# A talking-heads attention with a Fourier mix: the Fourier transform folded a second time, with other changes of order and transfer

## The chip, the cores and the metric

The kernel runs on one core of a Trainium2 chip. The metric is the time of one execution in device microseconds (us), and the median of several executions is taken. The core has five engines that work side by side, each with an instruction stream of its own: TensorE for matmuls (PE in the profile, with its loads of stationary weights as PEld), VectorE (DVE), ScalarE (ACT), GpSimd (POOL) and SyncE (SP), which here only issues transfers. Transfers are also issued by GpSimd, and with the change by ScalarE.

## What is computed

Everything is fp32. Attention over 8 batches, 12 heads, 448 rows and 64 elements per head is followed by a Fourier mix and a feed-forward block (cut):

```python
scores = scale * q @ k.T                           # b, h, i, j
scores = einsum('bhij,hg->bgij', scores, w_pre)    # "premix" over heads
attn = exp(scores - max) / (sum + 1e-09)
attn = einsum('bhij,hg->bgij', attn, w_post)       # "postmix" over heads
x = (attn @ v), heads side by side                 # 8 x 448 x 768
u = x + real(fft(fft(x, axis=1), axis=2))          # the Fourier mix
un = (u - mean) / sqrt(var + 1e-06)
out = u + relu(un @ w_ch1) @ w_ch2                 # 768 -> 3072 -> 768
```

The real part of the two transforms is cos(rows) x cos(columns) minus sin(rows) x sin(columns). Cosines are even and sines odd, so a row and its mirror image can be added or subtracted first, and only half the sums are needed: this is folding.

## The kernel before

The mixing phase goes through 192 steps, 24 for each batch. A step gathers scores for a few rows of all heads (Kr), mixes the heads (mx), takes maximum and exponential (PP), scales them on GpSimd, mixes again (po) and turns the result (Pv). Other work is dealt among the steps by the tables AT_*, counted from the start of a batch: transposes of q and k (AT_T), the scores (AT_QK), attention times v (AT_AV), transposes of the result into X (AT_X), the transform over rows (AT_Z, emit_z) and that over columns (AT_S, emit_s2). The pool named ms holds four PSUM tiles, mx has one of two banks. The Fourier work of a batch comes 14 or more steps after the batch has ended, and so among the steps of the next one.

X is folded once in each direction on GpSimd (pairs, even, odd). TensorE, VectorE and ScalarE take their instructions in the order of emission; GpSimd and SyncE get theirs from a scheduler. The result u goes to a DRAM tensor per batch; groups of rows that are held in reversed order are scattered to it row by row by an indirect transfer. After that a feed-forward phase reads u again. Weights are also split into parts and summed in advance (wts), one VectorE operation in a step.

```python
AT_T = ((7, 0), (18, 18), (15, 17))
AT_QK = ((0, 2, 2), (0, 1, 2), (0, 1, 2), (0, 1, 2),
         (0, 1, 2), (1, 1, 2), (0, 1, 2), (0, 1, 2))
AT_AV = ((0, 2, 4), (0, 1, 4), (3, 4, 5), (2, 3, 4))
AT_X = (11, 20, 25, 29)
AT_Z = (38, 38, 38, 38, 42, 42, 42)
AT_S = ((41, 44), (49, 53))
    # ... cut
    def emit_tables():
        for t, n in ((rows, "at"), (ts, "ts"), (tce, "tc"), (tdo, "td")):
            nc.sync.dma_start(out=t, in_=cn[n].ap())
    # ... cut
                nc.gpsimd.dma_start(
                    out=t[64 * y:64 * y + 64, :, x, :],
                    in_=src[b, 6 * y + 2 * xx + x].rearrange("(p c) d -> p c d", c=C7))
    # ... cut
    def emit_premix(T):
        mx = pmx.tile([P, 2, 512], F32, name="mx", tag="mx")
        Kr = steps[T]["Kr"]
        for x in range(2):
            for z in range(2):
                nc.tensor.matmul(mx[64 * z:64 * z + 64, x, :S],
                                 kw1[64 * x:64 * x + KR, :],
                                 Kr[64 * x:64 * x + KR, z, :], start=True, stop=True)
        steps[T]["mx"] = mx
    def emit_max(T):
        nmx = psm.tile([P, 2], F32, name="nmx", tag="nmx")
        for x in range(2):
            nc.vector.tensor_reduce(nmx[:, x:x + 1], steps[T]["mx"][:, x, :S],
                                    axis=AX.X, op=ALU.max, negate=True)
        steps[T]["nmx"] = nmx
    def emit_exp(T):
        PP = ppp.tile([P, 2, S], F32, name="PP", tag="PP")
        den = psm.tile([P, 2], F32, name="den", tag="den")
        for x in range(2):
            nc.scalar.activation(PP[:, x, :], steps[T]["mx"][:, x, :S], ACTF.Exp,
                                 bias=steps[T]["nmx"][:, x:x + 1],
                                 accum_out=den[:, x:x + 1])
        steps[T]["PP"], steps[T]["den"] = PP, den
    # ... cut
        for x in range(2):
            nc.gpsimd.tensor_scalar(PP[:, x, :], PP[:, x, :], rcp[:, x:x + 1], 1.0,
                                    op0=ALU.mult, op1=ALU.mult)
    # ... cut
        def pairs(op, h):
            if h == 0:
                box.append(pxs.tile([GR + 1, DM], F32, name="xs", tag="xs"))
            h = slice(h * DH, (h + 1) * DH)
            nc.gpsimd.tensor_tensor(box[-1][:n, h], Xa[:n, h], Xb[:n, h], op=op)
        def even():
            xs = box[-1]
            nc.gpsimd.tensor_copy(out=xe[:n, 0:DH + 1:DH], in_=xs[:n, 0:DH + 1:DH])
            nc.gpsimd.tensor_tensor(xe[:n, 1:DH], xs[:n, 1:DH], xs[:n, DM - 1:DH:-1],
                                    op=ALU.add)
        def odd():
            xd = box[-1]
            nc.gpsimd.tensor_tensor(xo[:n, :], xd[:n, 1:DH], xd[:n, DM - 1:DH:-1],
                                    op=ALU.subtract)
        folds.extend([lambda: pairs(ALU.add, 0), lambda: pairs(ALU.add, 1), even,
                      lambda: pairs(ALU.subtract, 0), lambda: pairs(ALU.subtract, 1),
                      odd])
        batches[g["b"]]["xf", pair] = (xe, xo)
    # ... cut
    def emit_z(b, par, ch):
        d0, w = (EVEN, ODD)[par][ch]
        ps = ms_tile()
        for pair, n in enumerate(PR):
            nc.tensor.matmul(ps[:w, :SH + 1],
                             batches[b]["xf", pair][par][:n, d0:d0 + w],
                             ts[:n, pair, par, :], start=(pair == 0), stop=(pair == 1))
        z = pzz.tile([w, SH + 1], F32, name=f"z{par}{ch}", tag=f"z{par}{ch}")
        batches[b]["z", par, ch] = z
        return [lambda: copy(ENG["z"], z[:, :], ps[:w, :SH + 1])]
    def emit_s2(b, pair, par):
        st = batches[b]
        n, i0 = PR[pair], pair * GR
        chunks, tab = ((EVEN, tce), (ODD, tdo))[par]
        ps = ms_tile()
        for ch, (_, w) in enumerate(chunks):
            nc.tensor.matmul(ps[:n, :DH + 1], st["z", par, ch][:, i0:i0 + n],
                             tab[:w, ch, :],
                             start=(ch == 0), stop=(ch == len(chunks) - 1))
        def done():
            for back in range(2):
                X = groups[b * NG + 2 * pair + back]["X"]
                m = GR if back else n
                sub, add = (ALU.subtract, ALU.add) if par else (ALU.add, ALU.add)
                if back:
                    sub, add = add, sub
                nc.vector.tensor_tensor(X[:m, 0:DH + 1], X[:m, 0:DH + 1],
                                        ps[:m, 0:DH + 1], op=sub)
                nc.vector.tensor_tensor(X[:m, DH + 1:DM], X[:m, DH + 1:DM],
                                        ps[:m, DH - 1:0:-1], op=add)
            if par == 0:
                return
            for back in range(2):
                X = groups[b * NG + 2 * pair + back].pop("X")
                if back:
                    nc.gpsimd.indirect_dma_start(
                        out=u_scr[b][:, :],
                        out_offset=bass.IndirectOffsetOnAxis(
                            ap=rows[:GR, pair:pair + 1], axis=0),
                        in_=X[:GR, :], in_offset=None)
                    continue
                nc.sync.dma_start(out=u_scr[b][i0:i0 + GR, :], in_=X[:GR, :])
                if n > GR:
                    nc.sync.dma_start(out=u_scr[b][i0 + GR:i0 + n, :], in_=X[GR:n, :])
        return [done]
    # ... cut
    ET = mybir.EngineType
    with tc.manual_schedule(engines={ET.PE, ET.DVE, ET.Activation}):
        while s < TOT or any(fill.values()):
            take("none", s)
            if 0 <= s + LM < TOT:
                emit_premix(s + LM)
                emit_max(s + LM)
            flush()
            if 0 <= s + LM < TOT:
                emit_exp(s + LM)
            if 0 <= s < TOT:
                emit_postmix(s)
            take("AV", s)
            if 0 <= s < TOT:
                emit_turn(s)
            if s >= 4:
                wts.deal(1)
            if 0 <= s + LM < TOT:
                emit_scale(s + LM)
            if folds:
                folds.pop(0)()
            take("QK", s)
            if 0 <= s + LG < TOT:
                if any(e[2] is not None and e[2] <= (s + LG) // BS for e in pend):
                    flush()
                emit_gather(s + LG)
            take("full", s)
            s += 1
        flush()
        wts.deal(1000)
    # ... cut
    def load_u(t):
        us[t] = pu.tile([P, NT2, DM], F32, name=f"u{t}", tag=f"u{t}")
        for x in range(NT2):
            p = 0
            while p < P:
                b, r = divmod(t * TB + x * P + p, S)
                n = min(P - p, S - r)
                nc.sync.dma_start(out=us[t][p:p + n, x, :], in_=u_scr[b][r:r + n, :])
                p += n
```

## Time and profile before

The time is 2514.99 us, the median of 3 executions (2512.84 to 2515.37). The profiled execution has a span of 2513.7 us.

| what | value |
|---|---|
| PE busy | 2412.0 us, 96% of the span |
| PEld busy | 1552.2 us, 62% |
| DVE, ACT, POOL busy | 1498.9, 794.2 and 636.0 us |
| mean granted clock of TensorE | 0.990 |
| moved by transfers | 373.01 MB, 148 GB/s |
| first premix (line 425) | starts at 48.69 us |
| first feed-forward matmul (line 834) | starts at 966.7 us |
| matmul instructions of emit_z (line 570) | 224 |
| matmul instructions of emit_s2 (line 584) | 224 |
| GpSimd additions of 384 elements (line 547) | 64 of 1003 ns |

How to read the profile: an engine's busy time counts from the start of an instruction to its end. Matmuls are pipelined, so that they overlap, and the distance between their starts tells more of their cost than their duration does. A row of a view in order of time has start, time taken, engine, line of the program, operation, the tile written and those read, and in brackets how long the engine was idle and what ended that. The chain follows what ended last back to what released it, step by step. "Issue" is time in which nothing that the profile shows was waited for.

### The profile page before, as it was taken

The numbers are of one execution on the slowest core, as the hardware profiler recorded it, in microseconds if no ns is written. First come the engines' busy times: TensorE is split into PE (matmuls) and PEld (weight loads), VectorE is DVE, ScalarE is ACT, GpSimd is POOL, SyncE is SP. The second block draws the span as 40 slices with busy tenths as digits, with TensorE's granted clock in tenths as the row PEclk, the third lists the DMA queues.
The fourth block names the chain that finished last, engine by engine and source line by source line (L and its number), as shares of the span: only waits on it lengthen the run. The fifth ranks groups of instructions, "written<-read, shape, count | busy, mean of one in ns | idle before, by whom it ended". The sixth has DMA issues, their size and how long they took to land.

```text
span 2513.7 us, 47590 instructions
## 1 busy us (share of the span) xinstructions
PE 2412.0 (96%) x18544; PEld 1552.2 (62%) x18544; DVE 1498.9 (60%) x3103; ACT 794.2 (32%) x2084; POOL 636.0 (25%) x1001
## 2 busy tenths in 40 slices
PE   4899999999999986999999999999999999999999
PEld 2344444444444455767777777777777777777776
DVE  1777777777777645786466536653665466533333
ACT  2676666666666622223111101110111011111110
POOL 5475665657564431111010000000000000000000
PEclk8999999999999988999999999999999999999999
DMA  5454544555553448343634443444444444443331
GB/s 155 141 173 153 166 159 154 167 168 167 171 160 128 143 143 274 118 146 114 224 123 150 151 155 128 145 151 158 132 145 147 158 131 145 134 152 116 129 113 51
DMA packets 154911, 373.01 MB, mean 148 GB/s; under 512 B 22471, under 2 KB 75719, under 8 KB 154688
## 3 DMA queue, kind: packets, MB, share of 16 engines
q1 hardware_dynamic: 123360, 260.63, 30.6%
q0 software_dynamic: 31328, 109.34, 14.6%
q8 instruction: 148, 2.42, 0.4%
q14 instruction: 75, 0.61, 0.1%
HBM read 212.96 MB, written 74.34 MB: 114 GB/s over the span
## 4 chain that ended last, share of the span: by engine, by line
PE 85%; DMA 3%; POOL 3%; ACT 3%; DVE 3%; issue 1%; SPq 1%; ACTq 0%; POOLq 0%; DVEq 0%
PE psP L834 17%; PE psP L888 17%; PE psR L834 9%; PE psR L888 9%; PE mx L425 5%; PE ms L489 5%; PE psQ L888 4%; PE psQ L834 4%; PE po L462 4%; PE ms L399 4%; PE ms L584 3%; DVE nmx L433 2%; ACT PP L441 2%; PE ms L570 2%; DMA Kr<-Sb 2%; POOL xs L547 1%
## 5 line engine op out<-in xcount | busy, mean ns | idle before, releaser
L834 PE MATMUL psP<-ub,w1t 128*128 128x256 f32 x2016 | 462.9, 379 | 0.0
L888 PE MATMUL psP<-w2t,h 128*128 128x384 f32 x1344 | 460.9, 486 | 0.0
L834 PEld LDWEIGHTS psP<-ub,w1t 128*128 128x128 f32 x2016 | 382.9, 190 | 60.7
L888 PEld LDWEIGHTS psP<-w2t,h 128*128 128x128 f32 x1344 | 254.4, 190 | 165.9
L182 POOL DMA_DIRECT2D raw<-in_moe_w_ch_dram x120 | 69.9, 583 | 996.8 <-DVE tmp L221 965.2
L441 ACT ACTIVATE PP<-mx,nmx 128x448 f32<-128x448 f32 x384 | 239.9, 629 | 259.6 <-DVE nmx L433 225.5
L433 DVE TENSOR_REDUCE nmx<-mx 128x1 f32<-128x448 f32 x384 | 221.7, 619 | 165.5 <-PE mx L425 165.1
L452 POOL TENSOR_SCALAR PP<-PP,rcp 128x448 f32<-128x448 f32 x384 | 240.3, 637 | 287.8 <-DVE rcp L450 228.0
L894 DVE TENSOR_TENSOR u<-u,psP 128x384 f32<-128x384 f32 x336 | 183.4, 552 | 143.6 <-PE psP L888 141.4
L839 ACT COPY h<-psP 128x512 f32<-128x512 f32 x42 | 24.6, 585 | 761.7 <-PE psP L834 721.6
L834 PE MATMUL psR<-ub,w1t 128*128 128x256 f32 x1008 | 231.4, 379 | 0.0
L888 PE MATMUL psR<-w2t,h 128*128 128x384 f32 x672 | 230.5, 486 | 0.0
L425 PE MATMUL mx<-Kr,kw 60*64 60x448 f32 x1536 | 194.5, 551 | 31.0 <-ACT PP L441 18.1
L473 DVE STREAM_TRANSPOSE Pv<-po 128x896 f32<-128x896 f32 x192 | 212.3, 1106 | 9.8 <-PE po L462 9.7
L845 DVE TENSOR_TENSOR h<-h,psQ 128x512 f32<-128x512 f32 x42 | 28.9, 688 | 300.7 <-PE psQ L834 295.3
L834 PEld LDWEIGHTS psR<-ub,w1t 128*128 128x128 f32 x1008 | 191.4, 190 | 26.3 <-DVE ub L813 0.3
L462 PE MATMUL po<-PP,kw 60*32 60x448 f32 x3072 | 190.3, 552 | 13.7 <-POOL PP L452 9.9
L399 PE MATMUL ms<-kT,qT 64*60 64x448 f32 (+1 forms) x1536 | 187.8, 561 | 7.9 <-DVE kT L285 7.9
L285 ACT COPY Sb<-ms 124x448 f32<-124x448 f32 x384 | 184.1, 541 | 10.1 <-PE ms L399 6.8
L489 PEld LDWEIGHTS ms<-Pv,vv 64*64 64x64 f32 x5376 | 143.2, 133 | 69.0 <-issue 27.1
L888 PEld LDWEIGHTS psR<-w2t,h 128*128 128x128 f32 x672 | 127.2, 190 | 87.4
L489 PE MATMUL ms<-Pv,vv 64*64 64x120 f32 x5376 | 165.6, 268 | 0.0
(92 smaller groups left out, 2632.7 us busy)
## 6 DMA issues: line engine op xcount, KB each, us to landing
ub<-ub SPq DMA_DIRECT2D x294, 384.0 KB
Kr<-Sb SPq DMA_DIRECT2D x768, 105.0 KB
raw<-in_moe_w_ch_dram POOLq DMA_DIRECT2D x72, 256.0 KB, 3.2
raw<-in_moe_w_ch_dram POOLq DMA_DIRECT2D x48, 384.0 KB, 3.6
w<-wst POOLq DMA_DIRECT2D x18, 896.0 KB, 4.7
w<-wst POOLq DMA_DIRECT2D x12, 1344.0 KB, 5.8
w1t<-w SPq DMA_DIRECT2D x42, 384.0 KB
w2t<-w SPq DMA_DIRECT2D x42, 384.0 KB
```

The lines of the kernel that those rows point to most:

```text
L285: (nc.scalar.copy if eng == "a" else nc.vector.tensor_copy)(out=out, in_=in_)
L399: nc.tensor.matmul(pss[x][64 * y:64 * y + r0 + 64 - lo, :S], st["qT", xx][64 * x:64 * x + 64, y, lo:r0 + 64], st["kT", xx][64 * x:64 * x + ...
L425: nc.tensor.matmul(mx[64 * z:64 * z + 64, x, :S], kw1[64 * x:64 * x + KR, :], Kr[64 * x:64 * x + KR, z, :], start=True, stop=True)
L433: nc.vector.tensor_reduce(nmx[:, x:x + 1], steps[T]["mx"][:, x, :S], axis=AX.X, op=ALU.max, negate=True)
L441: nc.scalar.activation(PP[:, x, :], steps[T]["mx"][:, x, :S], ACTF.Exp, bias=steps[T]["nmx"][:, x:x + 1], accum_out=den[:, x:x + 1])
L452: nc.gpsimd.tensor_scalar(PP[:, x, :], PP[:, x, :], rcp[:, x:x + 1], 1.0, op0=ALU.mult, op1=ALU.mult)
L462: nc.tensor.matmul(po[o:o + 32, z, :S], kw2[64 * z:64 * z + KR, y, :], PP[64 * z:64 * z + KR, :, c * HS:(c + 1) * HS], start=True, stop=True)
L473: nc.vector.transpose(g["Pv"][:, T % GT, :].rearrange("p (z s) -> p z s", z=2), steps[T]["po"][:, :, :S])
L489: nc.tensor.matmul(pss[y][64 * x:64 * x + 64, :nu * R], st["v", pr][64 * y:64 * y + 64, x, jb * D:(jb + 1) * D], _ap(Pv, 64 * y * rp + 32 ...
L834: nc.tensor.matmul(p[:, m, :], w1[i][:, kc, m * P:(m + 1) * P], ub[:, kc, :], start=i in OPENS and m == kc == 0, stop=kc == NK - 1, skip_g ...
L888: nc.tensor.matmul(p, lhs[i][:, kf, x * P:(x + 1) * P], w2[i][:, kf, :], start=i in OPENS and kf == 0, stop=kf == FM - 1, skip_group_check ...
L894: nc.vector.tensor_tensor(us_, us_, p, op=ALU.add)
```

## The change

It has five parts.

- The transform is folded a second time. Rows p and 224 - p are combined as well as rows p and 448 - p, and columns likewise, so that odd and even frequencies are separate sums with half the terms. For this the second pair of row groups is held in the reverse of the order it had. emit_z and emit_s2 have other shapes and write every second element of their PSUM tiles; GpSimd has more folding to do (sides, quarters, both). The tables of cosines and sines shrink.
- The rows that are held in reversed order go to DRAM tensors of their own, u_rev, so that scatters and straight stores of one batch no longer write to the same tensor. The feed-forward reads its rows from both.
- GpSimd takes its instructions in the order of emission. Scaling stands ahead of the folds of a step, at most two folds are emitted in a step, and stores come a step later (later).
- Transfers whose row count isn't a multiple of 16 are split into a part that is and the rest (_split).
- The q and k of the first batch are loaded by SyncE and ScalarE in turn, not by GpSimd. The cosine tables are emitted in step 3 on GpSimd, the first loads of weights no longer come first of all.

The tables AT_* are set anew, and in a step the postmix and the evacuations stand ahead of the maximum. The core of the diff (of the folds, emit_z and emit_s2 only the lines added and kept, for those removed stand above):

```diff
+DQ = DH // 2
+CW = DQ // 2 + 1
+FOLD = (((CW, CW - 1), (CW - 1, CW - 1)), ((CW - 1, CW - 1), (CW - 1, CW - 2)))
# ... cut
-AT_T = ((7, 0), (18, 18), (15, 17))
-AT_QK = ((0, 2, 2), (0, 1, 2), (0, 1, 2), (0, 1, 2),
-         (0, 1, 2), (1, 1, 2), (0, 1, 2), (0, 1, 2))
-AT_AV = ((0, 2, 4), (0, 1, 4), (3, 4, 5), (2, 3, 4))
-AT_X = (11, 20, 25, 29)
-AT_Z = (38, 38, 38, 38, 42, 42, 42)
-AT_S = ((41, 44), (49, 53))
-ENG = {("tr", "q", 4): "d", ("tr", "q", 3): "a", ("tr", "k", 4): "a",
-       ("tr", "k", 3): "d", "QK": "aa", "AV": "aa", "X": "aa", "z": "a"}
+AT_T = ((12, 10), (17, 16), (14, 18))
+AT_QK = ((1, 2, 2), (0, 1, 2), (0, 1, 2), (0, 1, 2),
+         (0, 1, 2), (0, 1, 2), (0, 1, 2), (0, 1, 2))
+AT_AV = ((0, 2, 3), (1, 3, 5), (3, 4, 5), (1, 2, 3))
+AT_X = (11, 20, 24, 29)
+AT_Z = (38, 38, 41, 41)
+AT_S = ((40, 44), (53, 55))
# ... cut
     def emit_tables():
-        for t, n in ((rows, "at"), (ts, "ts"), (tce, "tc"), (tdo, "td")):
-            nc.sync.dma_start(out=t, in_=cn[n].ap())
-        return []
+        for t, n in ((rows, "at"), (ts, "ts"), (tcs, "tc")):
+            for p, m in _split(0, t.shape[0]):
+                nc.gpsimd.dma_start(out=t[p:p + m], in_=cn[n].ap()[p:p + m])
# ... cut
+        for x in range(2):
+            eng = nc.gpsimd if b else (nc.sync, nc.scalar)[x]
+            eng.dma_start(
+                out=t[64 * y:64 * y + 64, :, x, :],
+                in_=src[b, 6 * y + 2 * xx + x].rearrange("(p c) d -> p c d", c=C7))
# ... cut
         def pairs(op, h):
             if h == 0:
+                box.append(pxs.tile([PN, DM], F32, name="xs", tag="xs"))
             h = slice(h * DH, (h + 1) * DH)
+            pl.tensor_tensor(box[-1][:, h], Xa[:, h], Xb[:, h], op=op)
# ... cut
+        def sides(par):
             xs = box[-1]
+            box[-1] = xs[:, 1:DH] if par else xs[:, :DH + 1]
+            pl.tensor_tensor(xs[:, 1:DH], xs[:, 1:DH], xs[:, DM - 1:DH:-1],
+                             op=ALU.subtract if par else ALU.add)
+        def quarters(par):
+            t, w, n = box[-1], DH + 1 - 2 * par, DQ - par
+            x = st["xq", par, pair] = pxf.tile([PN, w], F32, name="xq",
+                                               tag=f"xq{par}{pair}")
+            for c, op in ((0, ALU.add), (n + 1, ALU.subtract)):
+                pl.tensor_tensor(x[:, c:c + n], t[:, :n], t[:, w - 1:w - 1 - n:-1], op=op)
+            pl.tensor_copy(out=x[:, n:n + 1], in_=t[:, n:n + 1])
+        def both(par, r):
+            w = DH + 1 - 2 * par
+            if r == 0:
+                st["xf", par] = pxf.tile([PN, 2, w], F32, name="xf", tag=f"xf{par}")
+            pl.tensor_tensor(st["xf", par][:, r], st["xq", par, 0][:, :],
+                             st["xq", par, 1][:, :], op=(ALU.add, ALU.subtract)[r])
+        for par, op in enumerate((ALU.add, ALU.subtract)):
+            folds.extend([lambda op=op: pairs(op, 0), lambda op=op: pairs(op, 1),
+                          lambda par=par: sides(par), lambda par=par: quarters(par)])
+        if pair:
+            folds.extend(lambda par=par, r=r: both(par, r)
+                         for par in range(2) for r in range(2))
+    def emit_z(b, par, y):
+        while ("xf", par) not in batches[b] or folds:
+            folds.pop(0)()
+        w, at = FOLD[par][y]
+        c0 = (DQ - par + 1) * y
+        ps = ms_tile().rearrange("p (n q) -> p n q", n=2)
+        for n, d0 in enumerate((0, at)):
+            for r in range(2):
+                k = GR if par ^ r else PN
+                nc.tensor.matmul(ps[:w, n, r:SH + 1:2],
+                                 batches[b]["xf", par][:k, par ^ r,
+                                                       c0 + d0:c0 + d0 + w],
+                                 ts[:k, par, r, :PN - r], start=True, stop=True)
+        z = pzz.tile([CW, 2, SH + 1], F32, name=f"z{par}{y}", tag=f"z{par}{y}")
+        batches[b]["z", par, y] = z
+        return [lambda: copy(ENG["z"], z[:w, :, :], ps[:w, :, :SH + 1])]
     def emit_s2(b, pair, par):
         st = batches[b]
         n, i0 = PR[pair], pair * GR
         ps = ms_tile()
+        for y in range(2):
+            w, _ = FOLD[par][par ^ y]
+            for ch in range(2):
+                nc.tensor.matmul(ps[:n, y:DH + 1:2],
+                                 st["z", par, par ^ y][:w, ch, i0:i0 + n],
+                                 tcs[:w, par, y, ch, :DQ + 1 - y],
+                                 start=(ch == 0), stop=(ch == 1))
         def done():
             for back in range(2):
                 X = groups[b * NG + 2 * pair + back]["X"]
                 sub, add = (ALU.subtract, ALU.add) if par else (ALU.add, ALU.add)
                 if back:
                     sub, add = add, sub
+                nc.vector.tensor_tensor(X[:n, 0:DH + 1], X[:n, 0:DH + 1],
+                                        ps[:n, 0:DH + 1], op=sub)
+                nc.vector.tensor_tensor(X[:n, DH + 1:DM], X[:n, DH + 1:DM],
+                                        ps[:n, DH - 1:0:-1], op=add)
             if par == 0:
                 return
+            later.append(store)
+        def store():
             for back in range(2):
                 X = groups[b * NG + 2 * pair + back].pop("X")
+                if pair ^ back:
                     nc.gpsimd.indirect_dma_start(
+                        out=u_rev[b][:, :],
                         out_offset=bass.IndirectOffsetOnAxis(
                             ap=rows[:GR, pair:pair + 1], axis=0),
                         in_=X[:GR, :], in_offset=None)
+                    if pair:
+                        nc.sync.dma_start(out=u_rev[b][GR:GR + 1, :], in_=X[GR:GR + 1, :])
+                else:
+                    nc.sync.dma_start(
+                        out=u_scr[b][pair * (SH + 1):pair * (SH + 1) + GR, :],
+                        in_=X[pair:pair + GR, :])
         return [done]
# ... cut
-    with tc.manual_schedule(engines={ET.PE, ET.DVE, ET.Activation}):
+    with tc.manual_schedule(engines={ET.PE, ET.DVE, ET.Activation, ET.Pool}):
         while s < TOT or any(fill.values()):
-            take("none", s)
+            old = len(later)
+            n = take("none", s)
             if 0 <= s + LM < TOT:
                 emit_premix(s + LM)
-                emit_max(s + LM)
             flush()
-            if 0 <= s + LM < TOT:
-                emit_exp(s + LM)
             if 0 <= s < TOT:
                 emit_postmix(s)
+            if 0 <= s + LM < TOT:
+                emit_max(s + LM)
+                emit_exp(s + LM)
             take("AV", s)
             if 0 <= s < TOT:
                 emit_turn(s)
             if s >= 4:
                 wts.deal(1)
-            if 0 <= s + LM < TOT:
-                emit_scale(s + LM)
-            if folds:
-                folds.pop(0)()
             take("QK", s)
             if 0 <= s + LG < TOT:
                 if any(e[2] is not None and e[2] <= (s + LG) // BS for e in pend):
                     flush()
                 emit_gather(s + LG)
+            if 0 <= s + LM < TOT:
+                emit_scale(s + LM)
+            for _ in range(old):
+                later.pop(0)()
+            for _ in range(min(len(folds), 1 if n and s > 3 else 2)):
+                folds.pop(0)()
             take("full", s)
             s += 1
         flush()
+        while later:
# ... cut
-                n = min(P - p, S - r)
-                nc.sync.dma_start(out=us[t][p:p + n, x, :], in_=u_scr[b][r:r + n, :])
+                k = sum(r >= e for e in ENDS)
+                n = min(P - p, ENDS[k] - r)
+                src = (u_rev if k % 2 else u_scr)[b]
+                for p0, m in _split(p, n):
+                    nc.sync.dma_start(out=us[t][p0:p0 + m, x, :],
+                                      in_=src[r + p0 - p:r + p0 - p + m, :])
```

## The prediction

> **What bounds the kernel now.** I read the page's busy line first, then the busy time by stages, the granted clock in them, the chain of work that ended last, and for one batch the instructions in order of time.
>
> ```profile
> PE 2412.0 (96%) x18544; PEld 1552.2 (62%) x18544; DVE 1498.9 (60%) x3103; ACT 794.2 (32%) x2084; POOL 636.0 (25%) x1001
> ...
> 0.00:48.00 48.00, 18.16 (x82) 10.52 (x82) 6.58 (x19) 10.50 (x18) 27.70 (x51) 0.93 0.60 162
> 362.00:472.00 110.00, 106.67 (x1569) 51.00 (x1562) 78.68 (x168) 70.35 (x213) 67.43 (x107) 1.00 0.50 157
> 897.00:967.00 70.00, 43.73 (x491) 29.60 (x484) 27.50 (x61) 15.33 (x48) 22.35 (x32) 0.76 0.48 159
> 967.00:1100.00 133.00, 131.32 (x559) 98.71 (x558) 95.96 (x216) 38.47 (x66) 15.59 (x27) 1.00 0.54 185
> ```
>
> The columns are the stretch, its length, and busy time of PE, PEld, DVE, ACT, POOL, then clock, DMA share and GB/s. There are four stages: a start up to 48.7 us with PE mostly idle; the mixing phase, 192 steps in 8 batches, PE 97% busy; a passage of about 60 us with PE at 62% and a low clock; and from 967 us the feed-forward, PE 99% busy, which the change doesn't touch. So 1547 of 2514 us stay, and everything is decided in the first 967 us.
>
> In the mixing phase two things set a step. One is the work of PE. The other is a loop, seen in order of time:
>
> ```profile
> 331.60 0.98 PE L425 MATMUL mx<-Kr,kw 60*64 60x448 f32 x8
> 332.73 1.16 DVE L433 TENSOR_REDUCE nmx<-mx 128x1 f32<-128x448 f32 x2 [0.71 <-PE mx L425]
> 334.00 0.64 ACT L441 ACTIVATE PP<-mx,nmx 128x448 f32<-128x448 f32 x1 [0.81 <-DVE nmx L433]
> 334.62 0.62 ACT L441 ACTIVATE PP<-mx,nmx 128x448 f32<-128x448 f32 x1
> ```
>
> mx has one buffer, so the next premix waits for the exponentials: about 3.8 us from premix to premix, however little PE has to do. I took the distances of the premixes in the trace by step of the batch (means of batches 2 to 6). Steps with an AV block take 4.1, light ones 3.75 to 3.8, and those with Fourier work 6.25, 5.5, 6.0, 6.2, 5.8 and 5.5 (steps 1, 5, 14, 17, 18, 20). The sum is 108.8 us per batch; in batch 0, which has no Fourier work yet, it is 98.4. The work that I count for PE agrees: premix 0.9, postmix 0.9, QK 0.75, AV 1.65, a q/k transpose 0.77, an X transpose 0.66 us. So PE sets the heavy steps and the loop the light ones.
>
> The start and the passage, from the chain:
>
> ```profile
> 7.26 6.43 DMA rawq<-in_q_dram
> 17.11 8.98 DMA rawq<-in_q_dram
> 36.83 11.81 DMA Kr<-Sb
> 48.69 2.45 PE mx L425 x7
> ...
> 897.71 1.94 POOL xs L547 x2
> 905.30 1.26 POOL PP L452 x2
> 926.46 5.57 PE ms L570 x14
> 943.82 3.44 DMA u<-X,rows
> 947.40 0.32 SPq L610
> 948.53 6.13 DMA u<-u
> 966.91 0.43 PE psP L834 x2
> ```
>
> At the start the chain is loads, then a gather of 11.8 us, where later ones take 2 to 5. At 897 us the last scaling of PP stands behind folds on GpSimd, and at 943.8 a straight store waits for the scatter into the same tensor.
>
> **What the Trainium skill says.** "PSUM — Partial Sum Buffer", Specifications, gives 8-byte cachelines and says that any non-contiguous pattern slows matmuls significantly. The new transforms write every second fp32. No matmul here does that, so the trace can't say; this is my largest doubt. "DMA: Bandwidth & Descriptors", Why a DMA increments its semaphore by 16 and not by 1, says that a transfer uses the largest number of engines up to 16 that divides its outer dimension, so a prime number of rows goes over one. The trace agrees: while the 113-row table ts loads, the packets of the hardware queue sum to only 14 to 32 KB in each 2 us from 10 to 16 us and again from 26 to 38 us, and the slow gather stands in the same queue. The same page, Issuing engines are not separate DMA queues, says that several issuers save only issue time. Here that time counts: GpSimd needs 0.72 us for each 112 KB, an estimated 160 GB/s, and 116 to 212 GB/s are seen from 3 to 16 us. "GPSIMD Engine Reference", 3.1, has two-input operations at about 2.6 cycles per element; line 547 takes 1003 ns for 384, near 2.6 ns each with its dispatch.
>
> **The change part by part.** Matmuls first. An fp32 matmul is two instructions here, and the distance of their starts is 192 ns at 225 columns, 216 at 256, 326 at 385: columns/1.2 plus about 3 ns. Per batch:
> - z (line 570) has 14 matmuls, 28 x 192 ns = 5.4 us. After: 16 of 113 or 112 columns, 32 x 97 ns = 3.1 us, if weight loads keep up (transposes of 128 columns run at 109 ns each, so they do) and the stride costs nothing.
> - s2 (line 584) has 14, 28 x 326 = 9.1 us. After: 16 of 193 or 192 columns, 32 x 163 = 5.2 us.
>
> That is 6.2 us less PE work per batch, 50 us for 8. Not all of it comes through, for the loop floor remains. Placing the new table of steps: z at 14 and 17 (1.6 us each), s2 at 5, 7, 16, 20 (1.4 each). With 4.1 for AV steps (12, one of them with z), 3.8 for light ones, and 4.75, 4.1, 5.0, 4.75, 5.9, 4.7 for steps 5, 7, 14, 16, 17, 20, the 24 steps sum to 101 us. The same sum for before gives 106.7 where 108.8 was measured; the 2 us over came from stalls such as folds in front of a scaling (ACT waits for PP behind line 552, 11 times, 21 us in all). In emission order scaling goes first, so part of that should go; but now the maximum is emitted after the four additions of s2 (4 x 0.55 us, 2 us overlapped), which lengthens the loop by 1 us in up to three steps per batch. I take 103.3: 5.5 us less. Seven sets of z and s2 lie in the steps, the eighth in the passage: **-38 us**.
>
> GpSimd: folds are 12.4 us per batch now (8 x 1.0, 4 x 1.0, 2 x 0.2). After: per pair 4 whole-half additions of 1.0, two sides of 1.0, four quarter additions of about 0.5 and two copies of 0.1, 8.3 us; twice that and four combining additions of 1.0 give 20.6 us. GpSimd goes from 67 of 110 us to about 75 of 103: beside PE and not the bound.
>
> Start: 24 loads of 112 KB, 2.75 MB. Two hardware queues lift the issue limit; at 200 to 250 GB/s the last lands at 13 to 16 us, then transposes, QK and copies (5 us, clock cold) and a gather of 3 to 4 us, as the tables (before, 1.7 MB) and v now come behind the first scalings. The first premix should stand near 26 us in place of 48.7: **-22 us**.
>
> Passage: the last scaling no longer stands behind folds, -4.4 us. After the last X, before needs 3.3 us of folds to the first z; now eight folds and two combinations come first, about 11 us: +8. z and s2 take about 12 in place of 17 us: -5. The direct store still stands behind a one-row store that waits for the scatter, +1.5, and u's rows come in 12 pieces for 5 in the first tile, +1 (issue 0.46 us each, most under the transfers). Sum about **0**, with 4 us of doubt.
>
> Together 2515 - 38 - 22 = 2455.
>
> **Rivals.**
> 1. The strided PSUM write slows the new matmuls. At half rate z and s2 are 32 x 191 + 32 x 324 ns = 16.5 us, 2.0 more than now; the mixing phase gains nothing, and only the start is left: about 2500. For it: the page. [...] I give it one chance in five; a partial loss of 20 us is also possible.
> 2. The floor of 3.8 us or another engine takes over. In steps with s2, DVE has max 1.16, turn 1.1, additions 2.0 and small ones, about 5 us against 4.1 of PE. If that comes through four times a batch, some 15 us of the 38 are lost: 2470.
> 3. GpSimd in emission order becomes a wait: a load or scatter whose buffer isn't free holds the scaling behind it, and PE misses PP. Against it: scaling runs two steps ahead of its postmix, some 4 us of slack. If 2 us per batch: 2471. In the passage, folds of 12 us in a row could cost 5 us more than I took.
> 4. The start was bound by bytes of 256 and not by issue: then the loads end near 22 us and the start saves 14: 2463.
>
> **Range and chances.** The centre is 2455; the stride and the additions pull it up, so I say 2458. The low end takes -46 in the mixing phase, -26 at the start and some more in the passage; the high end the stride at more than half its cost. The 2% line is 2464.7, close to the centre: 0.59 for faster, 0.39 for the same, 0.02 for slower, which would need the stride and GpSimd's waits both.
>
> **What would show it.** First premix at 24 to 30 us, gather under 5 us. Starts of z instructions 97 ns and of s2 163 ns apart; nearer 190 and 320 would prove rival 1. Premix to premix summing to 101 to 105 us per batch, with steps 14 to 20 under 6 us. GpSimd near 690 us busy in all (636, 8 x 8.2 of folds more, 17 of load issues fewer) with no wait of line 462 on it in the steps. Last premix near 840 us, and 70 us from it to the first feed-forward matmul. A feed-forward phase other than 1547 us would be outside my reasoning, and so would a first premix after 35 us.

## The result, and the profile after

The changed kernel takes 2531.44 us (median of 4 executions, 2529.03 to 2533.17) against 2514.89 for the kernel before on the same chip (one execution more than in the 2514.99 above): ratio 1.0067, 95% interval 1.0049 to 1.0084. It is 0.7% slower; 2458 was predicted. The profiled execution has a span of 2531.2 us, 17.5 more than before.

The start went nearly as planned. The chain at the start, from the changed kernel's profile (start, time taken, what; line 439 is the gather, 449 the premix):

```profile
15.23 3.11 DMA rawq<-in_q_dram
...
18.57 1.73 PE ms L400 x7
...
23.17 3.02 PE ms L423 x24
...
28.62 3.56 DMA Kr<-Sb
```

The first premix starts at 28.6 us in place of 48.7: the loads end at 18.3, and the part of the first gather that is on the chain takes 3.6 us, where it was 11.8. But half of that premix waits for this part until 32.2, so the second premix comes 8.1 us after the first and not 5.5: it starts at 36.7 for 54.2, and by then the start is worth 17.5 us. The busy line of the page:

```profile
PE 2402.8 (95%) x18608; PEld 1547.6 (61%) x18608; DVE 1519.4 (60%) x3103; ACT 789.8 (31%) x2059; POOL 694.8 (27%) x1112
```

GpSimd is at 694.8 us, for 690 predicted. The distances from premix to premix show where the time went. The mean batch (2 to 6) now takes 112.9 us, where 108.8 was measured before and 103.3 predicted, and the last premix starts at 915.5 us, not near 840. These are the stretches of steps 4 and 5 of batch 3, first in the kernel before (columns as in the prediction: stretch, length, busy time of PE, PEld, DVE, ACT, POOL, clock, DMA share, GB/s):

```profile
389.29:393.37 4.08, 4.08 (x93) 2.25 (x88) 2.75 (x7) 2.90 (x12) 2.44 (x4) 1.00 0.85 221
393.37:398.89 5.52, 5.52 (x48) 2.37 (x40) 3.33 (x9) 3.64 (x11) 3.54 (x6) 1.00 0.56 145
```

and in the changed kernel:

```profile
389.41:393.22 3.81, 2.81 (x36) 0.59 (x28) 2.52 (x5) 2.62 (x10) 3.77 (x7) 1.00 0.93 214
393.22:403.32 10.10, 6.96 (x47) 3.03 (x47) 5.28 (x12) 3.25 (x9) 7.73 (x13) 1.00 0.96 209
```

Before, PE is busy all through; the transfer engines are at 85% in step 4 and at 56% in step 5. After, they are at 93 and 96%, and step 5 lasts 10.1 us, 3 of them with PE idle. The chain of the changed kernel names what it waits for:

```profile
393.17 0.87 ACT Sb L305 x2
...
396.48 13.29 DMA Kr<-Sb
```

A gather whose last part was issued at 396.48 landed 13.3 us later; the one before it, for step 6, had its last issue at 391.60 and let its premix start at 403.32. On the chain of the kernel before, the gathers of the mixing phase take 1.2 to 5.6 us from issue to landing. What fills the transfer engines is in the issues of the trace: in steps 3 to 5 the v of the batch (six transfers of 224 KB), as before the change, and in steps 2 to 5 now also the first of the q and k loads of the next batch. GpSimd's issues of loads in steps 3 to 5 of batch 3, before:

```profile
386.96 1.26 POOL L355 DMA_DIRECT2D vv<-in_v_dram  x2
...
390.83 1.24 POOL L355 DMA_DIRECT2D vv<-in_v_dram  x2
...
394.85 1.24 POOL L355 DMA_DIRECT2D vv<-in_v_dram  x2
```

and in the changed kernel, where a load of weights comes with them:

```profile
387.00 1.29 POOL L380 DMA_DIRECT2D vv<-in_v_dram  x2
388.27 1.49 POOL L372 DMA_DIRECT2D rawq<-in_q_dram  x2
389.74 0.59 POOL L201 DMA_DIRECT2D raw<-in_moe_w_ch_dram  x1
...
391.58 1.26 POOL L380 DMA_DIRECT2D vv<-in_v_dram  x2
392.84 1.43 POOL L372 DMA_DIRECT2D rawq<-in_q_dram  x2
...
395.56 1.28 POOL L380 DMA_DIRECT2D vv<-in_v_dram  x2
396.82 0.74 POOL L372 DMA_DIRECT2D rawq<-in_q_dram  x1
```

In the kernel before, GpSimd's scheduler had put the q/k loads of a batch into steps 1, 8, 9, 16 and 18 to 20, clear of v. In emission order they are issued where the code emits them, and that is counted from AT_T, which the change set anew.

Step times (means of batches 2 to 6, us), against the prediction's table:

| step | 1 | 5 | 7 | 13 | 14 | 16 | 17 | 20 | 22 | all 24 |
|---|---|---|---|---|---|---|---|---|---|---|
| predicted | 4.1 | 4.75 | 4.1 | 4.1 | 5.0 | 4.75 | 5.9 | 4.7 | 4.1 | 101 (103.3 taken) |
| after | 4.1 | 10.8 | 4.8 | 5.6 | 5.8 | 5.0 | 6.0 | 4.9 | 4.6 | 112.9 |

Step 5 alone holds 6.1 of the 11.9 us over the table's 101; in most other steps the table stands to within 0.3 us. Steps 13 and 14 are long in two batches, where VectorE waits for the first load of a group of weights. Batch 0 takes 113.0 us for 98.4 before; its step 5 alone takes 16.9, with v, the tables and batch 1's q and k all in the engines at once.

The passage, from the chain of the changed kernel (line 476 scales, 588 is the last fold, 611 and 627 are the transforms, 894 is the feed-forward's first matmul):

```profile
921.44 1.26 POOL PP L476 x2
...
945.40 1.00 POOL xf L588
...
951.51 1.57 PE ms L611 x16
...
953.69 1.58 PE ms L627 x8
...
961.78 3.60 DMA v<-X,rows
...
966.49 4.06 DMA u<-v
...
983.18 0.85 PE psP L894 x2
```

From the last premix to the first of these matmuls it is 67.5 us (70.1 before), and the feed-forward takes 1548.3 (1547.0 before): neither holds the loss.

### The profile page after: what moved, and what is told of

It reads as the page before. It is cut to its first block, busy times and chain, and to the rows that moved or that the text cites. A ratio compares the mean times of both kernels' runs of the same rounds, so it can differ in the third digit from the quotient of the medians.

```text
span 2531.2 us, 47914 instructions
## 1 busy us (share of the span) xinstructions
PE 2402.8 (95%) x18608; PEld 1547.6 (61%) x18608; DVE 1519.4 (60%) x3103; ACT 789.8 (31%) x2059; POOL 694.8 (27%) x1112
## 4 chain that ended last, share of the span: by engine, by line
PE 82%; DMA 6%; DVE 5%; ACT 4%; POOL 1%; issue 1%; SPq 1%; ACTq 0%; POOLq 0%; DVEq 0%
PE psP L894 17%; PE psP L948 17%; PE psR L894 9%; PE psR L948 9%; PE mx L449 6%; PE ms L513 5%; PE psQ L948 4%; PE psQ L894 4%; PE po L486 4%; DMA Kr<-Sb 4%; PE ms L423 3%; ACT PP L465 3%; DVE nmx L457 3%; PE ms L627 1%; PE ms L611 1%
## 5 line engine op out<-in xcount | busy, mean ns | idle before, releaser
L449 PE MATMUL mx<-Kr,kw 60*64 60x448 f32 x1536 | 216.3, 566 | 57.8 <-ACT PP L465 44.5
L423 PE MATMUL ms<-kT,qT 64*60 64x448 f32 (+1 forms) x1536 | 193.9, 564 | 5.5 <-DVE qT L305 5.5
L305 ACT COPY Sb<-ms 124x448 f32<-124x448 f32 x384 | 184.8, 541 | 18.3 <-DMA Kr<-Sb 12.5
```

Of the source, the lines that this page charges most:

```text
L305: (nc.scalar.copy if eng == "a" else nc.vector.tensor_copy)(out=out, in_=in_)
L423: nc.tensor.matmul(pss[x][64 * y:64 * y + r0 + 64 - lo, :S], st["qT", xx][64 * x:64 * x + 64, y, lo:r0 + 64], st["kT", xx][64 * x:64 * x + ...
L449: nc.tensor.matmul(mx[64 * z:64 * z + 64, x, :S], kw1[64 * x:64 * x + KR, :], Kr[64 * x:64 * x + KR, z, :], start=True, stop=True)
```

## The experiments

The versions were compared with the kernel before, run beside them on the same chip. Times are medians; batch means are those of batches 2 to 6 in the profiled execution.

**q and k earlier.** The loads of all batches but the first two get nine more steps of lead, those of batch 1 get five fewer, and the tables go from step 3 to 16, all to keep steps 2 to 5 clear.

```diff
-                due("none", max(old, f + a - GS - 9) + y,
+                due("none", max(old, f + a - GS - (9, 4, 18)[min(b, 2)]) + y,
-    due("none", 3, emit_tables)
+    due("none", 16, emit_tables)
```

> The changed kernel with one thing moved: the loads of the next batch's q and k come earlier (steps 16 to 23 and 12 to 15 of the batch before, as their buffers come free), so that none falls on steps 1 to 8, where v is loaded in steps 3 to 5; for the second batch they come in steps 6 to 15; the cosine tables come in step 16 and not 3. Theory T (collision of loads): the 16 DMA engines are full in steps 3 to 6, the gather Kr lands late and PE waits. T expects step 5 to fall from 10.8 to about 4.8 us, step 5 of batch 0 from 16.9 to under 6, the last premix from 915 to about 865 us, the time to 2470 to 2490 us. Theory R1 (the one-row store that waits for the scatter blocks the gathers behind it in SyncE's queue) and theory R2 (GpSimd in emission order makes waits of its own) expect step 5 to stay over 8 us and the time over 2515.

Measured: 2517.66 us, ratio 1.0015 (1.0008 to 1.0023), so 14 us less than the changed kernel. Step 5 falls to 8.1, batch 0's to 8.4, the batch to 110.2. The direction is right, the size a quarter to a third of the 41 to 61 us that T expected: in steps 4 and 5 the transfer engines stay at 85 and 86%, with v still there. As numbers, a step 5 over 8 us and a time over 2515 are what R1 and R2 expected; the next two runs put these to the test.

**The single row out of the scatter's tensor.** In the changed kernel SyncE's store of one row waits for the scatter into the same tensor, up to 3.4 us at a time, with gathers behind it.

```diff
-ENDS = (GR, GR * 2 + 1, GR * 3 + 1, S)
+ENDS = (GR + 1, GR * 2 + 1, GR * 3 + 1, S)
-                        nc.sync.dma_start(out=u_rev[b][GR:GR + 1, :], in_=X[GR:GR + 1, :])
+                        nc.sync.dma_start(out=u_scr[b][GR:GR + 1, :], in_=X[GR:GR + 1, :])
```

> The changed kernel with row 112 of each batch stored to the tensor of straight rows, so that no store in SyncE's queue waits for a scatter. R1 expects the 29.8 us that SyncE waits at that store to come back as time: about 2505 us, with step 5 under 8 us. T expects nothing in the steps (step 5 stays near 10.8) and only the 3 to 4 us of the last store before the feed-forward: 2524 to 2530 us.

Measured: 2536.54, ratio 1.0091 (1.0068 to 1.0115), step 5 at 10.8 as ever. The wait is gone and nothing came of it: it was no cause, and R1 is wrong.

**GpSimd back to the scheduler**, everything else as changed.

```diff
-    with tc.manual_schedule(engines={ET.PE, ET.DVE, ET.Activation, ET.Pool}):
+    with tc.manual_schedule(engines={ET.PE, ET.DVE, ET.Activation}):
```

> The changed kernel with GpSimd handed back to the scheduler, as in the kernel before; everything else is as changed. R2 expects the loss to vanish with the emission order: under 2490 us, no step over 7 us. T expects the time to follow where the scheduler puts the loads: if the DMA share in steps 3 to 6 stays over 0.8, step 5 stays over 8 us; if it falls, it gets faster. The start should lose its gain (first premix after 35 us) if v and tables then come ahead of the first gather again.

Measured: 2577.69, ratio 1.0249 (1.0222 to 1.0277), 46 us more than the changed kernel. What PE waits for in that run, in the mixing phase and just after (total us, times, longest):

```profile
PE po L486 <- POOL PP L476: 60.0, 14, 7.5
```

Step 5 is milder (6.6): in this run the q and k loads are issued in steps 11 to 20, and none in 2 to 5. But now scaling stands behind folds, which are more than before, and the postmix waits for it; and the first premix starts at 37.7. So R2 is wrong: with the folds and tables of the change, the scheduler's order costs more than the emission order does.

**First weight load of a group a step earlier**: issued with the last part of the group before, not after its store.

```diff
# ... cut
-        self.ops.append((lambda: [load(k) for k in range(self.ahead)], False))
+        self.nexts.append(lambda: [load(k) for k in range(self.ahead)])
+        mine = len(self.nexts)
+        if mine == 1 or not self.hoist:
+            self.ops.append((self.nexts[mine - 1], False))
         for k in range(len(ps)):
             self.ops.append((lambda k=k: begin(k), True))
+            if k == len(ps) - 1 and self.hoist:
+                self.ops.append((lambda: len(self.nexts) > mine and self.nexts[mine](), False))
```

> The changed kernel with the first weight load of each group issued with the last part of the group before (28 steps of use later than its buffer is free, but some 10 steps earlier than now), in place of right after the store of that group. Theory R3: in emission order this load comes one step ahead of its first use, and VectorE, in order, waits for it: 21.3 us in 4 waits. R3 expects these waits to vanish and the time to fall by 15 to 20 us, to about 2513. T expects half of that, as a load that lands in a quiet step needs 3 us and is in time anyway; step 5 of most batches stays over 9 us.

Measured: 2528.02, ratio 1.0053 (1.0032 to 1.0073), 3.4 us less. That is short of the 8 to 20 of the two theories, and the interval overlaps that of the changed kernel. In the changed kernel VectorE's waits in the mixing phase have this row:

```profile
DVE tmp L218 <- DMA raw<-in_moe_w_ch_dram: 35.5, 5, 14.2
```

and with the earlier load this one:

```profile
DVE tmp L220 <- DMA raw<-in_moe_w_ch_dram: 15.5, 1, 15.5
```

Four of five waits are gone (the one left, at 75 us, is that of the first group), step 13 falls from 5.6 to 4.75, and step 5 stays at 10.9.

**v spread.** Its loads in halves over steps 2 to 7, and q and k where the change has them.

```diff
# ... cut
-            due("none", f + AT_AV[-1][pr] + 2, lambda b=b, pr=pr: emit_load_v(b, pr))
+            for y in range(2):
+                due("none", f + 2 + 2 * pr + y, lambda b=b, pr=pr, y=y: emit_load_v(b, pr, y))
```

> After, with the twelve half loads of v (112 KB each) of a batch issued one or two per step over steps 2 to 7 in place of four per step in steps 3 to 5; the q/k loads stay where they are. Theory T (the gather of step 5 is late because v and the next batch's q/k are in the same engines): DMA share of steps 4 and 5 falls from 0.94 and 0.91 to about 0.8, step 5 from 10.8 to 7 to 8 us, the batch from 112.9 to about 110, the whole to 2505 to 2515 us. Rival U (the q/k loads alone fill the engines, v doesn't matter): step 5 stays above 10 us, whole 2528 to 2534. Rival X (the stall is a wait of an engine and not of transfers): no step changes, 2531.

Measured: 2522.34, ratio 1.0038 (1.0021 to 1.0055), step 5 at 8.8, the batch at 111.3: 9 us less, where 16 to 26 were expected.

**Both: q and k earlier, v spread.**

> After, with both: q/k loads of batches from the third on issued nine steps earlier (steps 16 to 23 and 12 to 15 of the batch before), tables at step 16, and v spread over steps 2 to 7. T: nothing but v's halves is left in steps 2 to 7, DMA share there 0.5 to 0.65, step 5 under 5.5 us, the batch at 106 to 107, last premix 870 to 880, the whole 2490 to 2500 us. U: no better than with the q/k loads moved alone, 2515 to 2519. X: step 5 above 8 us, the whole 2515 or more.

Measured: 2502.82, ratio 0.996 (0.9948 to 0.9972), step 5 at 6.2, the batch at 108.2. Where the two moves alone gave 14 and 9 us, together they give 29, and the kernel is faster than before. It is 3 us short of the expectation: step 5 still takes 9.7 us in batch 4.

**Both, and the weights.**

> The same two moves and the first weight load of each group issued with the last part of the group before. T: 3 us below the version with the two moves, 2487 to 2497 us, which beats both kernels. If weights are only waits beside other work: the same as the two moves within 1 us.

Measured: 2486.28, ratio 0.9901 (0.9878 to 0.9923), the batch at 106.8, batch 1 at 101.8 for 110.7. The weights, worth some 3 us alone, are worth 16 on top. The gains don't add, for a step is freed only when all that crowds it has gone.

**v left out.** The changed kernel without the v loads of batches 1 to 7; their AV products take batch 0's v, so this is another computation and only a measure of what these transfers cost.

```diff
-                        st["v", pr][64 * y:64 * y + 64, x, jb * D:(jb + 1) * D],
+                        batches[0]["v", pr][64 * y:64 * y + 64, x, jb * D:(jb + 1) * D],
-            due("none", f + AT_AV[-1][pr] + 2, lambda b=b, pr=pr: emit_load_v(b, pr))
+            if b == 0:
+                due("none", f + AT_AV[-1][pr] + 2, lambda b=b, pr=pr: emit_load_v(b, pr))
```

> After, with the v loads of batches 1 to 7 left out (their AV products use batch 0's v, so the output is another one); 1.3 MB per batch less, everything else as in after. T: DMA share of steps 3 to 6 falls below 0.65 and step 5 of batches 1 to 7 to 4.8 to 5.5 us; 7 times 5.5 us less: 2490 to 2495 us. U (q/k loads alone do it): step 5 still above 8 us, 2515 or more. X: no change, 2531.

Measured: 2505.9, ratio 0.9965 (0.9956 to 0.9974), 25 us less, for the 36 to 41 expected: batch 0, which keeps its v, takes 114.2 us. Nothing but bytes was taken away, no instruction of PE, VectorE or ScalarE, and step 5 goes from 10.8 to 6.1 (4.9 in two of the five batches; batch 4 keeps 10.1). Batch 3, where nothing else collides, is at the predicted sum:

```profile
356.88:459.77 102.89, 100.57 (x1570) 49.84 (x1574) 83.67 (x167) 69.71 (x212) 72.01 (x114) 1.00 0.45 145
```

**A heavier step 1.** In steps 2 to 5 the last issue of a gather lies 7.1 to 8.4 us ahead of its premix in the kernel before, and only 4.4 to 5.6 in the changed one, since step 1 has become 2 us shorter. This run puts s2 of the second pair back into steps 1 and 5. It moves no load, but the stores of u, which follow s2, come three steps earlier (in steps 6 to 8, for 9 to 11).

```diff
-AT_S = ((40, 44), (53, 55))
+AT_S = ((40, 44), (49, 53))
```

> After, with AT_S back at ((40, 44), (49, 53)): the second pair's transforms over columns stand in steps 1 and 5, as before, and not in 5 and 7; no transfer is moved. Theory L (the gathers of steps 2 to 6 are late because step 1 has become light: their last issue lies about 4 to 5 us ahead of the premix, where the kernel before had 7 to 8): step 1 takes 0.6 to 0.9 us longer, the gathers get that much lead, and step 5 falls from 10.8 by 1 to 2.5 us; 8 to 14 us less in all, 2517 to 2524 us. Rival E (the transfers alone decide, lead doesn't matter): steps 1 and 7 change places in cost, step 5 stays at 10 to 11, 2528 to 2534 us.

Measured: 2532.49, ratio 1.0073 (1.0056 to 1.009): no gain over the changed kernel. The lead did come back (6.3 to 7.5 us in steps 2 to 5), and step 5 took 4.9 us in three of five batches; but step 7 then took 5.7 to 9.2 in four of them. The chain of that run, at step 7 of batch 3:

```profile
398.85 9.97 DMA Kr<-Sb
...
408.87 1.75 PE mx L449 x2
```

A late gather now stands two steps on. Here the longer lead changed which step pays, and not what is paid in all. The earlier stores may have a part in step 7, but in the version with all moves, below, they stand in the same steps and step 7 takes 3.7 us.

**Emission order alone, in the kernel before.**

```diff
-    with tc.manual_schedule(engines={ET.PE, ET.DVE, ET.Activation}):
+    with tc.manual_schedule(engines={ET.PE, ET.DVE, ET.Activation, ET.Pool}):
```

> Before, with GpSimd in emission order and nothing else. Theory C (emission order is good in itself, for scaling goes ahead of folds): 5 to 15 us faster, 2500 to 2510. Theory D (emission order is only good in company with the new tables and the load split; alone it puts q/k, v and weight loads back into the steps 2 to 5 where the scheduler had taken them out): 10 to 40 us slower, 2525 to 2555, with a stall in steps 4 to 6.

Measured: 2571.32, ratio 1.0224 (1.0207 to 1.0241), 57 us slower, more than the 40 of theory D, and the batch at 118.3. I had the sign but not the place: the stall is in step 12 (10.1 us). The q and k loads are issued in steps 23, 0, 8, 10 to 12 and 16 of this run and not in 2 to 5, so the crowd of the changed kernel doesn't come from emission order alone: it takes the new tables as well. GpSimd in that run, in order of time:

```profile
318.77 2.84 POOL L345 DMA_DIRECT2D rawq<-in_q_dram  x4
321.61 2.77 POOL L345 DMA_DIRECT2D rawk<-in_k_dram  x4
324.41 1.25 POOL L452 TENSOR_SCALAR PP<-PP,rcp 128x448 f32<-128x448 f32 x2
```

and PE in the same view:

```profile
325.72 1.75 PE L462 MATMUL po<-PP,kw 60*32 60x448 f32 x16 [4.15 <-POOL PP L452]
```

Eight issues, 5.6 us, stand ahead of a scaling, and the postmix waits 4.15 us for it.

**The same with q and k in halves**, a half to a step, as the change deals them:

```diff
# ... cut
-            due("none", max(old, f + a - GS - 8),
-                lambda b=b, xx=xx, nm=nm: emit_load_qk(b, xx, nm))
+            for y in range(2):
+                due("none", max(old, f + a - GS - 8) + y,
+                    lambda b=b, xx=xx, nm=nm, y=y: emit_load_qk(b, xx, nm, y))
```

> Before, with GpSimd in emission order and each q/k load dealt in two halves to two steps, as the change has it. In the run with emission order alone, step 12 had eight load issues of 0.71 us in a row ahead of a scaling and took 10 us. Theory H (the blocks of issues in front of the scaling are the cost): steps 12 to 14 lose 6 to 8 us per batch, 2510 to 2530 us. Theory S (the wait of the scatter for the straight store, 43 us in all, is the larger part): 2540 us or more.

Measured: 2561.31, ratio 1.0202 (1.0177 to 1.0228). Step 12 falls to 6.2 but step 13 rises to 6.8, and the batch is at 115.2. The blocks of issues were worth 10 us at most, not the 40 and more that H says; beside the kernel before it is 1.0202 for 1.0224, and the intervals overlap.

**And with the scattered rows in tensors of their own** (cut: the scatter writes to u_rev, and load_u reads rows from 225 on there, without splitting into multiples of 16):

```diff
# ... cut
-                        out=u_scr[b][:, :],
+                        out=u_rev[b][:, :],
-                n = min(P - p, S - r)
-                nc.sync.dma_start(out=us[t][p:p + n, x, :], in_=u_scr[b][r:r + n, :])
+                e = SH + 1 if r <= SH else S
+                n = min(P - p, e - r)
+                src = (u_scr if r <= SH else u_rev)[b]
+                nc.sync.dma_start(out=us[t][p:p + n, x, :], in_=src[r:r + n, :])
```

> The same, with the scattered rows in DRAM tensors of their own, read back from there. H: 0 to 8 us less than with the halves alone. S: 25 us less or more.

Measured: 2558.1, ratio 1.0195 (1.0167 to 1.0223), no clear gain, though the scatter's wait for the straight store is gone, so S, as put, is wrong as well. The mixing phase does gain: the last premix comes at 922.6 us and not at 937.5. But the passage and the feed-forward give 16 us back, 78.0 us for 69.2 and 1555.1 for 1547.6, for the rows now come in pieces of 97, 31 and the like. The chain in that passage:

```profile
979.16 16.27 DMA u<-ur
995.44 1.04 ACT un L799
```

So, by this chain, the split into multiples of 16 belongs to the separate tensors; no run adds the split alone. Emission order still costs the old kernel some 33 us in its mixing phase (last premix 922.6 for 896.7, from a start 6.9 us earlier); steps 13 of batches 1 and 5 take 13 and 15 us there, and VectorE's wait for weights stands at 31.8 us, as in the changed kernel, which suggests the first weight loads for part of it. The rest I leave open.

**All moves, and s2 in step 1.** This asks whether the longer lead helps once the crowd is thin.

> The version with q/k loads, v loads and first weight loads moved, and AT_S back at ((40, 44), (49, 53)). Little is left to stall in step 5 there (6.0 against 4.9 us undisturbed), so L expects 0 to 8 us less than 2486, and E 0 to 3 us more or less.

Measured: 2484.83, ratio 0.9885 (0.9868 to 0.9901); the interval overlaps that of the version without it, so the time doesn't tell L from E. In the profiled execution step 5 takes 4.9 us in every one of batches 2 to 6 and the batch 105.6. Steps 4 and 5 of batch 3 of that version:

```profile
370.69:374.50 3.81, 2.81 (x36) 0.58 (x28) 2.49 (x5) 2.62 (x10) 2.17 (x5) 1.00 0.83 239
374.50:379.40 4.90, 4.90 (x48) 2.62 (x48) 3.58 (x10) 3.24 (x9) 2.35 (x4) 1.00 0.39 106
```

The transfer engines are at 83% in one step and at 39% in the next (85 and 56% before the change), and PE has no idle time left in step 5.

**The old order of maximum and exponential**, in the version with q, k, v and weights moved: maximum ahead of the evacuations, exponential ahead of the postmix, which is rival 2 of the prediction put to the test.

```diff
                 emit_premix(s + LM)
+                emit_max(s + LM)
             flush()
+            if 0 <= s + LM < TOT:
+                emit_exp(s + LM)
             if 0 <= s < TOT:
                 emit_postmix(s)
-            if 0 <= s + LM < TOT:
-                emit_max(s + LM)
-                emit_exp(s + LM)
```

> The version with q/k loads, v loads and first weight loads moved, with the order in a step as before: maximum ahead of the evacuations, exponential ahead of the postmix. Theory M (the four additions ahead of the maximum lengthen the loop in steps with columns' transforms, rival 2 of the prediction): steps 5, 7, 16 and 20 are 0.3 to 1 us shorter, 2478 to 2484 us. Rival N (the new order keeps PSUM tiles free for TensorE, which the old order delays): steps with evacuations get longer, 2490 us or more. Within 2 us of 2486: the order doesn't matter.

Measured: 2488.0, ratio 0.9899 (0.9883 to 0.9916), against 2486.28 and 0.9901 with the new order. Steps 7, 16 and 20 are the same to 0.05 us; step 5 differs only in batches in which it stalls. The order doesn't matter here.

**All moves, without v.** The version with q, k, weights and s2 moved, v of batches 1 to 7 left out as above: what is left of transfers?

> The version with q/k loads, first weight loads and the s2 of step 1 moved, with the v loads of batches 1 to 7 left out (their AV products use batch 0's v, so the output is another one). Of the 76 us that the kernel lies over the prediction's sum, the moves gave some 45 back; this asks what the rest is. Theory T (still transfers): batches 2 to 6 fall from 105.6 to 103.5 or less, the whole to 2470 us or less. Theory W (steps are now at their own work and loop, and what is left stands in batch 0): batches 2 to 6 at 104.5 to 105.6, batch 0 still 107 or more, the whole 2476 to 2485 us.

Measured: 2485.91, ratio 0.9899 (0.9873 to 0.9924), the same as with all of v. Batches 2 to 6 take 105.3 us for 105.6, as theory W has it, though the whole is 1 us over W's range. Once placed, v costs 0.3 us in such a batch. Batch 0, in which v is loaded here in one block again, takes 112.7 for 107.5 with v spread, which hides in the total what the other batches gain.

## Why the prediction was wrong

The sum of the prediction's own terms is 2452.4 us before its rounding (26 to the first premix, batches of 98.4, 101, five of 103.3 and 93.5 us, of which the first is the one measured before and 101 and 93.5 are those before less 5.5, then 70 and 1547). Set beside the profiled executions (us):

| term | predicted | after | difference | all moves, s2 in step 1 | difference |
|---|---|---|---|---|---|
| first premix | 26 | 28.6 | +2.6 | 28.3 | +2.3 |
| batch 0 | 98.4 | 113.0 | +14.6 | 107.5 | +9.1 |
| batch 1 | 101.0 | 110.7 | +9.7 | 101.5 | +0.5 |
| batches 2 to 6 | 5 x 103.3 | 5 x 112.9 | +48.0 | 5 x 105.6 | +11.5 |
| batch 7, to its last premix | 93.5 | 98.8 | +5.3 | 98.6 | +5.1 |
| passage | 70 | 67.5 | -2.5 | 68.2 | -1.8 |
| feed-forward | 1547 | 1548.3 | +1.3 | 1548.2 | +1.2 |

- **The step that failed** is the one that reads "the 24 steps sum to 101 us ... I take 103.3: 5.5 us less", -38 us in all. It gave each step the larger of PE's work and the loop, and so took every gather to be in time. I had seen in the windows of the kernel before that the transfer engines were half used, and that was a mean: I didn't place the loads of q, k, v and weights by step in the new order of GpSimd. In their place the runs showed gathers that land late in a crowd of loads: step 5 took 10.8 us for 4.75, and the batch 112.9 for 103.3. Moving those loads and the cosine tables, and nothing of the arithmetic, brings the time from 2531 to 2486 us, 45 of the 73 us between prediction and result; leaving v out gives 25 of them without touching any engine's work. Both show the cause of the larger part.
- **Emission order** was looked at for one danger only, that GpSimd would hold scaling back (rival 3, "a load or scatter whose buffer isn't free"). In the changed kernel it doesn't: in the mixing phase no postmix matmul waits for a scaling, and no weight load of a postmix for more than 1.4 us. It does in the old kernel, where blocks of issues make a postmix wait 4.15 us, and the change had its remedies on board, loads in halves and tensors of their own. What emission order did here, together with the new tables, was to fix when transfers start.
- **The start** was right in size: -20.1 us for -22 by the first premix, -17.5 by the second. But "the tables ... and v now come behind the first scalings" counted only what left the start. They landed in batch 0, which lost 14.6 us; moving them gave 5.5 of these back. The loads ended at 18.3 us, between the 13 to 16 of the estimate and the 22 of rival 4, so that rival may be true in part.
- **PE's work** was right: the starts of z instructions are 98 ns apart and of s2 165 (97 and 163 predicted), and 16 of line 611 take 1.57 us in the passage above. Rival 1, at one chance in five, the stride in PSUM, is refuted. The page of the Trainium skill "PSUM — Partial Sum Buffer", Specifications, has any non-contiguous pattern slow matmuls significantly; for fp32 with a stride of two elements the measurement decides.
- **Rival 2**, the maximum behind the additions, was judged by turning the order back: 2488.0 for 2486.3, no effect.
- **What is left** even with all moves, 28 us: 9 in batch 0, of which 2.5 are the first premix that waits for its gather, while for the rest I suspect tables, v and q/k of batch 1, which still have to come in together; 2.3 us in each of batches 2 to 6, which is 4.6 over the table's 101 (step 1, which has s2 in this version, is 1.6 over, and steps 13, 14, 16 and 22 are 0.4 to 0.8 over); and 5 in batch 7, which I took to gain like the others though it lies at 98.8 for 99.0 before. Leaving v out lowers batches 2 to 6 by 0.3 us only, so v isn't it. Which work it is there I did not take apart.
- **The passage**: -2.5 us against 0, within the doubt named, though its parts were off and partly made up for each other. By the two chains it is -2.7 up to the end of the last scaling (-4.4 reckoned), +3.9 from there to z (+8) and -3.8 from z to the feed-forward (-2.5). The folds on GpSimd that precede its transforms end at 946.4, 23.7 us after the last scaling, some of them beside matmuls of the last steps.

With the transfers placed, then, the mean batch goes from 108.8 to 105.6 us and the whole to 2484.83, 1.2% under the kernel before (0.9868 to 0.9901). How much of that is the folding's isn't shown, for no run has the folding alone: 20 us are the earlier first premix. By the distances of their starts, z and s2 take an estimated 8.4 us of PE in a batch for 14.5 (32 x 98 + 32 x 165 ns against 28 x 192 + 28 x 326).

## What to carry to other kernels

When an engine that also issues transfers is taken from a scheduler and put in emission order, and the tables that date its loads are set anew, the loads come at other times: make a table of bytes and DMA share by step, and keep every bulk load out of the steps in which a gather on the critical loop has little lead. A mean DMA share of a half says nothing of this. A step that becomes faster also shortens the lead of the transfers that feed the next ones, here from 7.1 to 8.4 us to 4.4 to 5.6. Try such moves together, since one alone may only leave the crowd to the others: 14, 9 and 3 us alone were 45 together.

## What the hardware showed that was not expected

- fp32 matmuls that write every second element of a PSUM row run as fast as dense ones: 98 ns for 113 columns, 165 ns for 193, on the same line (columns / 1.2 + 3 ns) as the dense ones before, 192 ns for 225.
- Where a gather stands on the chain, its part of 105 KB took 1.2 to 5.6 us from issue to landing in the mixing phase of the kernel before, and up to 13.3 us in the changed one. The five that took 9.7 us or more there had the transfer engines at 81 to 98% in that time. A high share alone doesn't say it, though: at 85% another took 4.6 us.
- Rows in pieces of 97 and 31 made the read of u wait 16.3 us for its last part, where the longest read on the changed kernel's chain takes 4.1. It fits what the Trainium skill says in "DMA: Bandwidth & Descriptors", Why a DMA increments its semaphore by 16 and not by 1: a transfer runs on the largest number of engines up to 16 that divides its rows, which for 97 or 31 rows is one. In the stretch from 965 to 1000 us, cut into 40 slices, many move only 25 GB/s:

```profile
GB/s 249 39 42 284 225 337 284 77 28 25 28 25 25 84 312 225 204 211 344 144 98 98 116 25 81 298 116 25 25 147 305 39 25 25 25 25 25 25 25 28
```
